# Taking a scheduled kernel into hand-made issue order: HGRN2 attention and an ELU MLP on one TensorE

## The chip, the cores and the metric

The kernel runs on one core of one Trainium2 chip. The metric is the device time of one execution in microseconds (us); where several executions are compared, the median is given with the lowest and the highest, and the number of executions. Engines are called as in the profile: PE is TensorE's matmul, PEld its weight load, DVE is VectorE, ACT is ScalarE, POOL is GpSimd, SP issues the DMAs. The granted clock is the share of TensorE's full clock that the profile records.

## The reference

The program computes a gated linear attention (a decaying 48x48 state for each head) and feeds its output as tokens into a two-layer MLP with ELU.

```python
q, k, v, f_logit          # (4, 8, 768, 48) float32 each
x     : tokens 3072, d_model 384, d_ff 2048
# attention
f = 1 / (1 + exp(-f_logit))
for t in range(768):
    state = f[:, :, t, :, None] * state + k_t outer v_t
    y[:, :, t] = q_t @ state
# MLP on x = y as (3072, 384)
h = x @ w_in                                   # 384 -> 2048
g = where(h > 0, h, exp(min(h, 0)) - 1)
return (g @ w_out).astype(float32)             # 2048 -> 384
```

The two weight matrices are float32 draws multiplied by a float64 scalar, so they arrive as 64-bit words. The kernel makes 32-bit weights of them itself; that is the "word split" below.

## The kernel before

The program works on 12 units of 256 tokens. In the outer loop, stage m runs the MLP of unit m and, threaded between its steps, the attention of unit m+1. Each of a stage's 16 steps is an "up" (six float32 matmuls into `psH`, two records each in the trace, so x12; then ACT, ACT and DVE make `gg`, and from the third stage on four DVE sums prepare the next operand) or a "down" (`psM`).

```python
def up(P):
    m, j = divmod(P, NP)
    ph = ps.tile([128, 2, U], FP32, tag="h", name=f"psH{m}_{j}", bufs=2)
    ...                                                       # six matmuls psH <- wi, xt: 2 tiles x 3 rows
    nc.scalar.activation(g[:], ph[:], AF.Relu, scale=-1.0)
    nc.scalar.activation(g[:], g[:], AF.Exp, scale=-1.0)
    nc.vector.scalar_tensor_tensor(out=g[:], in0=g[:], scalar=-1.0, in1=ph[:], op0=ALU.add, op1=ALU.max)
    if m >= DIRECT:                                           # DIRECT = 2
        ...                                                   # four tensor_tensor "sums"
```

The attention of a unit: decays (scan, reciprocal, product for each of four head pairs), transposes of k, `advance` (the outer products, into the PSUM banks a0 and a1), the chunk states on DVE, `scores` (again a0 and a1) with the causal mask, and `outputs` (a0 and a1 once more). So these three groups of matmuls take turns at the same two banks. The DVE instructions stood inside the functions whose matmuls they follow:

```python
def scores(u):
    ...                                       # 32 matmuls psS (64 records)
    for r in range(2):
        nc.vector.tensor_tensor(...)          # the mask, right behind the scores

def advance(u):
    ...                                       # 32 matmuls psU (64 records)
    for c in range(NC - last):
        stepped(u, c, ...)                    # the state operations, right behind them

def attention(u):
    return {
        3: [lambda: transposed(u, 0, "a0"), lambda: transposed(u, 1, "a1")],
        6: [lambda: advance(u)],
        8: [lambda: scores(u)],
        10: [lambda: outputs(u)],
        12: [lambda: carried(u)],
    }
```

The word split of one weight tile has one ACT and three DVE instructions:

```python
nc.scalar.activation(raw.bitcast(I32)[:, 0::2], raw.bitcast(U32)[:, 0::2], AF.Copy, scale=2.0**-29)
nc.vector.tensor_scalar(out=bits[:], in0=hi, ..., op0=ALU.logical_shift_left, op1=ALU.bitwise_and)
nc.vector.tensor_tensor(out=bits[:], in0=bits[:], in1=rnd, op=ALU.add)
nc.vector.scalar_tensor_tensor(out=to.bitcast(I32), in0=rows(hi), scalar=-(2**30), in1=rows(bits[:]),
                               op0=ALU.bitwise_and, op1=ALU.bitwise_or)
```

Issue order is made by hand in the preamble and stage 0 alone. From there the scheduler may move instructions on each engine:

```python
start.enter_context(tc.manual_schedule())
...                       # preamble
for m in range(NU):
    ...
    if m == 0:
        start.close()     # the scheduler orders what follows
        combine()
```

Of the kernel before, what the change touches and what calls it, by code (L numbers as in the profile page):

```python
# [10 lines left out]
U32 = mybir.dt.uint32  # L11
AF = mybir.ActivationFunctionType
# [343 lines left out]
def fast(ctx: ExitStack, tc: tile.TileContext, q, k, v, f_logit, w_in, w_out, out, flag):  # L356
# [14 lines left out]

# [17 lines left out]
    DIRECT = 2  # L389
    AHEAD = 7  # L390
# [35 lines left out]
    start.enter_context(tc.manual_schedule())  # L426
    blank(0, nc.vector, nc.gpsimd)
    load(0, nc.scalar)

    ident = cst.tile([128, 128], FP32, name="ident")  # L430
# [14 lines left out]
    for i in range(1, NB):  # L445
        blank(i, nc.gpsimd)
    between = cst.tile([128, NW, HP], FP32, name="between")
    fine = cst.tile([128, HP, NC], FP32, name="fine")
    nc.vector.memset(fine[:], 1.0)
    py = ps.tile([128, HP, W], FP32, tag="a1", name="psY")  # L450
    nc.vector.memset(py[:], 0.0)
# [15 lines left out]
    parts = [(0, 0), *((j + i, 1 - i) for j in range(NFT // 2 - 1) for i in (1, 0)), (NFT // 2 - 1, 1)]  # L467
# [19 lines left out]
    def rounding(n):  # L487

        if wide and n < NFT:
            raw = raws[n]  # L490
            nc.scalar.activation(
                raw.bitcast(I32)[:, 0::2], raw.bitcast(U32)[:, 0::2], AF.Copy, scale=2.0**-29
            )

    def convert(n):





        if not wide or n >= NFT:
            return
        j, out_ = parts[n]
        raw = raws.pop(n)
        rnd = raw.bitcast(I32)[:, 0::2]
        hi = raw.bitcast(I32)[:, 1::2]
        bits = sb.tile([128, 2 * DM], I32, tag="bits", name=f"bits{n}", bufs=1)
        nc.vector.tensor_scalar(
            out=bits[:], in0=hi, scalar1=3, scalar2=0x3FFFFFF8,
            op0=ALU.logical_shift_left, op1=ALU.bitwise_and,  # L510
        )
        nc.vector.tensor_tensor(out=bits[:], in0=bits[:], in1=rnd, op=ALU.add)
        to = wo[:, 2 * j : 2 * j + 2] if out_ else wi[:, :, j * 256 : (j + 1) * 256]

        def rows(x):
            return x.rearrange("p (k f) -> p k f", k=to.shape[1])

        nc.vector.scalar_tensor_tensor(
            out=to.bitcast(I32), in0=rows(hi), scalar=-(2**30), in1=rows(bits[:]),
            op0=ALU.bitwise_and, op1=ALU.bitwise_or,  # L520
        )
# [4 lines left out]

    def check(n):

        if not wide:
            return  # L530
        w = w_out if n % 2 else w_in
        flat = w.rearrange("a b -> (a b)").rearrange("(p i f) -> i p f", p=128, f=2 * DM)
        raw = area[:, 4 + n % (AHEAD - 4)]
        nc.sync.dma_start(out=raw, in_=flat[n // 2])
        for i, op in enumerate((ALU.min, ALU.max)):
            nc.vector.tensor_reduce(  # L536
                out=spans[:, i, n : n + 1], in_=raw.bitcast(FP32)[:, 1::2], axis=mybir.AxisListType.X,
                op=op, apply_absolute_value=True,
            )


    restart = cst.tile([128, HP, U], FP32, name="restart")
    nc.gpsimd.memset(restart[:], 0.0)

    def gates(u):
# [3 lines left out]
        for i in range(2):  # L549
            a = f[:, 2 * i : 2 * i + 2] if u else f[:, :, i * W : (i + 1) * W]  # L550
            nc.scalar.activation(a, a, AF.Exp, scale=-1.0)
            nc.scalar.activation(a, a, AF.Copy, bias=1.0)
            if u:
                nc.gpsimd.tensor_copy(restart[:, 2 * i : 2 * i + 2, ::C], a[:, :, ::C])
                nc.gpsimd.memset(a[:, :, ::C], 0.0)  # L555

    def growth(u, pairs, cols):

        t = qkf[u % NB]
        for p in range(pairs.start, pairs.stop):  # L560
            a = t["f"][:, p, cols]
            nc.vector.tensor_tensor_scan(  # L562
                out=a, data0=a, data1=restart[:, p, cols] if u else a,
                initial=1.0, op0=ALU.mult, op1=ALU.max,
            )
        k_ = t["k"][:, pairs, cols]
        nc.gpsimd.tensor_tensor(out=k_, in0=k_, in1=t["f"][:, pairs, cols], op=ALU.mult)  # L567

    def decays(u, pairs, cols):

        t = qkf[u % NB]
        nc.vector.reciprocal(pts[u][:, pairs, cols], t["f"][:, pairs, cols])  # L572
        q_ = t["q"][:, pairs, cols]
        nc.vector.tensor_tensor(out=q_, in0=q_, in1=pts[u][:, pairs, cols], op=ALU.mult)
# [7 lines left out]
    def prepare(u):  # L582

        gates(u)
        yield
        for i in range(2):
            for p in range(2 * i, 2 * i + 2):
                growth(u, slice(p, p + 1), slice(0, U))
            yield
        for p in range(HP):  # L590
            decays(u, slice(p, p + 1), slice(0, U))
            yield
        watch(u)

    def transposed(u, w, bank):

        pt = ps.tile([128, HP, 128], FP32, tag=bank, name=f"psT{u}_{w}")
        for p in range(HP):
            nc.tensor.transpose(pt[:, p, :], in_=qkf[u % NB]["k"][:, p, w * W : (w + 1) * W], identity=ident[:])  # L599
        kns[u, w] = sb.tile([128, HP, 128], FP32, tag="kn", name=f"kn{u}_{w}")  # L600
        nc.scalar.copy(kns[u, w][:], pt[:])

    def stepped(u, c, pu, end):

        s = sb.tile([128, HP, D], FP32, tag="state", name=f"state{u}_{c}", bufs=6)
        now = pu
        if u % UPB or c:
            nc.vector.tensor_tensor(out=s[:], in0=pu, in1=sts[u, c][:], op=ALU.add)
            now = s[:]
        decay = pts[u][:, :, end - 1 : end].broadcast_to([128, HP, D])  # L610
        nc.vector.tensor_tensor(out=s[:], in0=now, in1=decay, op=ALU.mult)
        sts[(u, c + 1) if end < U else (u + 1, 0)] = s

    def scores(u):
# [3 lines left out]
        pc = [ps.tile([128, NW, HP, C], FP32, tag=f"a{r}", name=f"psS{u}_{r}") for r in range(2)]  # L618
        for w in range(NW):
            for p in range(HP):  # L620
                for b in range(2):
                    cols = slice(w * W + b * C, w * W + b * C + C)
                    for r in range(2):
# [3 lines left out]
                        )  # L627
        for r in range(2):
            nc.vector.tensor_tensor(
                out=at[:, r].rearrange("k w p i -> k (w p) i"), in0=pc[r][:].rearrange("k w p i -> k (w p) i"),  # L630
# [3 lines left out]
    def advance(u):  # L634

        last = u % UPB == UPB - 1
        pu = [ps.tile([128, NW, HP, D], FP32, tag=n, name=f"psU{u}_{n}") for n in ("a0", "a1")]
        for w in range(NW):
            for p in range(HP):
                for r in range(2):  # L640
                    h = 2 * p + r
                    for b in range(2):
                        nc.tensor.matmul(  # L643
                            pu[b][FULL[r], w, p], lhsT=kns[u, w][FULL[b], p, FULL[r]],
# [3 lines left out]
        for c in range(NC - last):  # L648
            stepped(u, c, pu[c % 2][:, c // 2], (c + 1) * C)

    def outputs(u):


        pys[u] = [ps.tile([128, NW, HP, C], FP32, tag=f"a{b}", name=f"psY{u}_{b}") for b in range(2)]
# [41 lines left out]
    def first_scores(w):  # L696
        t = qkf[0]
        cols = slice(w * W, (w + 1) * W)
        at = ats[0, w] = sb.tile([128, 2, HP, W], FP32, tag="at", name=f"at0_{w}")
        pc = [ps.tile([128, HP, W], FP32, tag=f"m{2 + r}", name=f"psS0_{w}_{r}") for r in range(2)]  # L700
        for p in range(HP):
            for r in range(2):
                nc.tensor.matmul(
                    pc[r][:, p], lhsT=t["k"][HALF[r], p, cols], rhs=t["q"][HALF[r], p, cols],
                    start=True, stop=True,
                )
        for r in range(2):
            nc.vector.tensor_tensor(
                out=at[:, r], in0=pc[r][:], in1=causal[:].unsqueeze(1).broadcast_to([128, HP, W]),
                op=ALU.mult,  # L710
            )

    def first_advance(w):
        pu = ps.tile([128, HP, D], FP32, tag="a0", name=f"psU0_{w}")
        for p in range(HP):
            for r in range(2):
                h = 2 * p + r
                nc.tensor.matmul(
                    pu[FULL[r], p], lhsT=kns[0, w][:, p, FULL[r]], rhs=vs[0][:, w, h * D : (h + 1) * D],
                    start=(p == 0), stop=(p == HP - 1), skip_group_check=True,  # L720
                )
        stepped(0, w, pu[:], (w + 1) * W)

    def first_outputs(w):





        cols = slice(w * W, (w + 1) * W)  # L730
        q_ = qkf[0]["q"]
        if w == 0:
            xts[0] = sb.tile([128, HP, U], FP32, tag="xt", name="xt0", bufs=3)
        at = ats.pop((0, w))
        for part in range(2 if w else 1):
            for i in range(2 * NKT):
                j, r = divmod(i, 2)
                n = slice((j - 1) * PAD, (j + 1) * PAD)
                v0 = (2 * NKT + r) * D
                nc.tensor.matmul(  # L740
                    py[64 * r + 32 : 64 * r + 64, j, :],
# [241 lines left out]
```

## Time and profile before

| | before |
|---|---|
| median of 3 runs | 623.61 us (621.86 to 624.21) |
| span of the profiled execution | 620.9 us |
| PE busy | 572.7 us (92%) |
| first up | 33.9 us |
| stage 0, stage 1 | 65.7 and 62.6 us |
| a late stage | 44.9 us, PE busy 44.90 |

The prediction below shows the busy shares, the slices and three stretches. Two more views matter for what follows. The first is the fine timeline of a late stage before, DVE alone; the columns are start in us, length in us, engine, line, operation, tiles and shapes, and in brackets idle time before it and what ended it.

```profile
362.35 0.36 DVE L608 TENSOR_TENSOR state<-psU_a,state 128x192 f32<-128x192 f32 x1 [0.34 <-PE psU_a L643]
...
367.23 0.63 DVE L797 SCALAR_TENSOR_TENSOR gg<-gg,psH 128x512 f32<-128x512 f32 x1
...
370.51 1.27 DVE L629 TENSOR_TENSOR at<-psS,twice 128x512 f32<-128x512 f32 x2
...
373.70 0.63 DVE L797 SCALAR_TENSOR_TENSOR gg<-gg,psH 128x512 f32<-128x512 f32 x1
```

The reader should see the order. The state operations, which read `psU_a` and start at 362.35, come ahead of the next `gg` (367.23), and the mask (370.51) ahead of the one after (373.70). Both banks are free long before PE wants them, as the PE timeline of the same stage shows, where no bracket stands:

```profile
367.29 1.16 PE L624 MATMUL psS<-q,k 48*64 48x64 f32 x64
...
373.45 1.16 PE L661 MATMUL psY<-at,v 64*64 64x64 f32 x64
```

The second is from the table of costly groups: the up (count, busy us, mean ns of one, idle time before it).

```profile
L790 PE MATMUL psH<-xt,wi 128*128 128x256 f32 x1152 | 275.2, 390 | 0.0
```

The up never waited for anything that the group counts (the last column is 0.0). The ACT conversion of 768 words (the old word split) took 900 ns in the median of its 16 instances (870 to 940).

### The profile page before, as it was taken

How to read it: one execution, taken by the hardware profiler on the slowest of the kernel's cores; microseconds unless marked ns; L12 is line 12 of the kernel's file. 1: busy time of each engine (PE TensorE's matmuls, PEld its weight loads, DVE VectorE, ACT ScalarE, POOL GpSimd, SP SyncE). 2: the span in 40 equal slices, each digit the busy share in tenths (PEclk: the TensorE clock that was granted, in tenths of full speed). 3: DMA queues.
4: the chain of work that ended last, by engine and by line, in shares of the span. 5: the costliest groups of instructions: out<-in, count | busy, mean ns of one | idle time of the engine just before them, and what ended most of it. 6: DMA issues, size and time to landing. Idle time of an engine off the chain costs nothing.

```text
span 620.9 us, 13009 instructions
## 1 busy us (share of the span) xinstructions
PE 572.7 (92%) x5402; PEld 499.3 (80%) x5402; DVE 413.4 (67%) x839; ACT 196.7 (32%) x352; POOL 59.1 (10%) x115
## 2 busy tenths in 40 slices
PE   2787699898999899999999999999999999999994
PEld 1556476675879899899999899999989989999993
DVE  6879999998699976667576675483493443532432
ACT  2254244233413323325314322323313313323220
POOL 7021003223001001002002001000000000000000
PEclk9887799979999999999999999999999999999998
DMA  8999709338682403003112112002000000000000
GB/s 187 250 253 246 184 3 197 64 84 261 221 279 79 159 32 87 26 26 86 44 28 69 41 27 59 27 26 59 25 2 8 26 2 8 26 3 8 27 0 31
DMA packets 31781, 50.78 MB, mean 82 GB/s; under 512 B 3520, under 2 KB 24544, under 8 KB 31712
## 3 DMA queue, kind: packets, MB, share of 16 engines
q1 hardware_dynamic: 31088, 49.26, 30.0%
q8 instruction: 44, 0.72, 0.5%
q10 hardware_dynamic: 624, 0.59, 0.4%
q14 instruction: 25, 0.20, 0.1%
HBM read 44.04 MB, written 4.72 MB: 79 GB/s over the span
## 4 chain that ended last, share of the span: by engine, by line
PE 69%; DVE 14%; DMA 8%; issue 5%; POOL 1%; ACT 1%; SPq 0%; DVEq 0%; POOLq 0%
PE psH L790 33%; PE psM L840 25%; DMA area<-in_moe_w_in_dram 5%; DVE p L572 4%; PE psM L818 3%; DVE f L562 3%; DMA q<-in_q_dram 2%; PE psS L624 2%; DVE spans L536 2%; PE psU_a L643 2%; DVE gg L797 2%; PE psY L661 1%; PE psT L599 1%; PE psY L681 1%; DMA f<-in_f_logit_dram 1%
## 5 line engine op out<-in xcount | busy, mean ns | idle before, releaser
L790 PE MATMUL psH<-xt,wi 128*128 128x256 f32 x1152 | 275.2, 390 | 0.0
L790 PEld LDWEIGHTS psH<-xt,wi 128*128 128x128 f32 x1152 | 218.8, 194 | 32.2
L797 DVE SCALAR_TENSOR_TENSOR gg<-gg,psH 128x512 f32<-128x512 f32 x96 | 64.8, 676 | 162.5 <-ACT gg L796 132.4
L795 ACT ACTIVATE gg<-psH 128x512 f32<-128x512 f32 x96 | 57.2, 596 | 323.6 <-PE psH L790 299.2
L840 PE MATMUL psM<-area,sums 128*128 128x192 f32 x480 | 91.3, 326 | 0.0
L572 DVE RECIPROCAL p<-f 128x256 f32<-128x256 f32 x48 | 82.5, 1734 | 0.3
L840 PEld LDWEIGHTS psM<-area,sums 128*128 128x128 f32 x480 | 80.2, 190 | 0.0
L840 PE MATMUL psM<-wo,gg 128*128 128x192 f32 x320 | 65.5, 327 | 3.5 <-DVE gg L797 3.5
L840 PEld LDWEIGHTS psM<-wo,gg 128*128 128x128 f32 x320 | 55.4, 190 | 8.3 <-DVE gg L797 4.7
L567 POOL TENSOR_TENSOR k<-k,f 128x256 f32<-128x256 f32 x48 | 39.7, 853 | 230.0 <-DMA k<-in_k_dram 196.0
L796 ACT ACTIVATE gg<-gg 128x512 f32<-128x512 f32 x96 | 60.6, 631 | 2.6
L818 PE MATMUL psM<-wo,gg 128*128 128x384 f32 x128 | 47.3, 516 | 3.3 <-DVE gg L797 3.3
L807 DVE TENSOR_TENSOR sums<-gg 128x128 f32<-128x128 f32 x160 | 42.5, 306 | 2.0
L818 PEld LDWEIGHTS psM<-wo,gg 128*128 128x128 f32 x128 | 25.3, 203 | 19.4 <-DVE gg L797 4.1
L562 DVE TENSOR_TENSOR_SCAN f<-f,restart 128x256 f32<-128x256 f32 x44 | 31.6, 761 | 11.6 <-POOL f L555 11.6
L840 PE MATMUL psM<-area,gg 128*128 128x192 f32 x160 | 39.1, 326 | 0.0
L840 PE MATMUL psM<-wo,sums 128*128 128x192 f32 x160 | 39.1, 326 | 0.0
L599 PE MATMUL psT<-ident,k 128*128 128x128 f32 x96 | 15.3, 298 | 18.3 <-POOL k L567 18.3
L536 DVE TENSOR_REDUCE spans<-area 128x1 f32<-128x768 f32 x32 | 29.3, 942 | 2.0 <-DMA area<-in_moe_w_out_dram 1.7
L599 PEld LDWEIGHTS psT<-ident,k 128*128 128x128 f32 x96 | 12.0, 151 | 21.3 <-POOL k L567 20.0
L840 PEld LDWEIGHTS psM<-area,gg 128*128 128x128 f32 x160 | 28.1, 190 | 0.1
L840 PEld LDWEIGHTS psM<-wo,sums 128*128 128x128 f32 x160 | 28.1, 190 | 0.0
(79 smaller groups left out, 427.5 us busy)
## 6 DMA issues: line engine op xcount, KB each, us to landing
area<-in_moe_w_out_dram SPq DMA_DIRECT2D x16, 768.0 KB, 7.7
area<-in_moe_w_in_dram SPq DMA_DIRECT2D x8, 768.0 KB, 5.9
v<-in_v_dram SPq DMA_DIRECT2D x12, 384.0 KB, 4.4
area<-in_moe_w_in_dram SPq DMA_DIRECT2D x16, 288.0 KB, 9.0
f<-in_f_logit_dram SPq DMA_DIRECT2D x23, 192.0 KB, 4.3
k<-in_k_dram SPq DMA_DIRECT2D x23, 192.0 KB, 3.9
q<-in_q_dram SPq DMA_DIRECT2D x23, 192.0 KB, 3.6
out_dram<-o SPq DMA_DIRECT2D x10, 384.0 KB, 2.5
```

Of the source, the lines that this page charges most:

```text
L536: nc.vector.tensor_reduce(out=spans[:, i, n : n + 1], in_=raw.bitcast(FP32)[:, 1::2], axis=mybir.AxisListType.X, op=op, apply_absolute_val ...
L562: nc.vector.tensor_tensor_scan(out=a, data0=a, data1=restart[:, p, cols] if u else a, initial=1.0, op0=ALU.mult, op1=ALU.max,)
L567: nc.gpsimd.tensor_tensor(out=k_, in0=k_, in1=t["f"][:, pairs, cols], op=ALU.mult)
L572: nc.vector.reciprocal(pts[u][:, pairs, cols], t["f"][:, pairs, cols])
L599: nc.tensor.transpose(pt[:, p, :], in_=qkf[u % NB]["k"][:, p, w * W : (w + 1) * W], identity=ident[:])
L790: nc.tensor.matmul(ph[:, i], lhsT=wi[:, kt, n : n + 128], rhs=xts[m][:, kt, :], start=(kt == 0), stop=(kt == NKT - 1),)
L795: nc.scalar.activation(g[:], ph[:], AF.Relu, scale=-1.0)
L796: nc.scalar.activation(g[:], g[:], AF.Exp, scale=-1.0)
L797: nc.vector.scalar_tensor_tensor(out=g[:], in0=g[:], scalar=-1.0, in1=ph[:], op0=ALU.add, op1=ALU.max)
L807: nc.vector.tensor_tensor(out=s[:, i], in0=x, in1=y, op=op)
L818: nc.tensor.matmul(pm[t][:], lhsT=g[:, i, t * 128 : (t + 1) * 128], rhs=wo[:, 2 * j + i, :], start=(j == 0 and i == 0), stop=(j == NP - 1 ...
L840: nc.tensor.matmul(pm[bank][:, half * DH : (half + 1) * DH], lhsT=x, rhs=y, start=first, stop=(j == NP - 1), skip_group_check=True,)
```

## The change

The intent: place every instruction of the whole program by hand, so that the front, where DVE is the full engine, can be packed more tightly. The parts are these.

- `manual_schedule` is closed only at the end of the program.
- Decays, state operations and the mask become functions with steps of their own (0 to 3, 7 and 9). Downs lag two ups behind instead of one.
- Unit 0 goes through the four-chunk form of the other units; the padding rows between its heads come from zero-padded columns.
- The word split is cut in two: `split` (two DVE instructions with one source each, one ACT conversion with a 16-bit output) and, a step or more later, `merge` (a 32-bit add that writes the weights).
- Smaller matters: the activation table is loaded first, the last output goes out in smaller writes, the banks of a down are taken in another order, `combine` is spread over stage 1, and the re-reading of weights for the range check is separated from the check.

```diff
+    nc.scalar.preload_act_table(AF.Exp)
...
-        nc.vector.tensor_tensor(out=bits[:], in0=bits[:], in1=rnd, op=ALU.add)
+        nc.vector.tensor_scalar(out=hi, in0=hi, scalar1=-(2**30), scalar2=None, op0=ALU.bitwise_and)
+        nc.scalar.activation(
+            raw.bitcast(U16)[:, 2::4], raw.bitcast(U32)[:, 0::2], AF.Copy, scale=2.0**-29
+        )
+
+    def merge(n):
...
-        nc.vector.scalar_tensor_tensor(
-            out=to.bitcast(I32), in0=rows(hi), scalar=-(2**30), in1=rows(bits[:]),
-            op0=ALU.bitwise_and, op1=ALU.bitwise_or,
-        )
+        nc.vector.tensor_tensor(out=to.bitcast(I32), in0=rows(bits[:]), in1=rows(hi), op=ALU.add)
...
     def attention(u):
+        kept = []
         return {
-            3: [lambda: transposed(u, 0, "a0"), lambda: transposed(u, 1, "a1")],
+            **{p: [lambda p=p: decays(u, p)] for p in range(HP)},
+            4: [lambda: watch(u)],
+            5: [lambda: transposed(u, 0, "a0"), lambda: transposed(u, 1, "a1")],
             6: [lambda: advance(u)],
-            8: [lambda: scores(u)],
+            7: [lambda c=c: step(u, c) for c in range(NC)],
+            8: [lambda: kept.append(scores(u))],
+            9: [lambda: mask(u, kept[0])],
             10: [lambda: outputs(u)],
...
             P = m * NP + s // 2
+            if m == 0:
+                split(s + 3)
+                merge(s + 2)
             for f in todo.get(s - (m == 0), ()):
                 f()
             if s % 2 == 0:
                 up(P)
-            elif P:
-                down(P - 1)
+            elif P >= LAG:
+                down(P - LAG)
...
-        if m == 0:
-            start.close()
-            combine()
...
-    down(NU * NP - 1)
+    for P in range(NU * NP - LAG, NU * NP):
+        down(P)
+    start.close()
```

## The prediction

Statements about the hardware that the trace of the kernel before does not show are cut from the prediction, each cut marked. Its sum: 141 + 537.5 + 5.2 + 8.5 = 692.2 us of span, 695 with the 2.7 of the offset, 715 with the 20 for the clock (not quite half of the 46, an estimate from the one gap of 2.15 us told there). DVE's order: the L508, L512 and L518 of a tile of stage 0 start at 54.22, 54.91 and 55.91 us. That each engine keeps the order of issue (step 4) was the premise. The clock: "did not" means that it stayed at 1.00, after 1.11 us of idle before 106.97 and after 1.33 before 252.56; but after 1.34 us before 180.43 the scores ran at 1.00 and the up behind them, from 183.2, at 0.53. The 1.28 us at 5.28 is the load of the activation table.

> **What bounds the kernel now.** The program works on 12 units of 256 tokens. Stage m runs the MLP of unit m in 16 steps: even steps are an "up" (12 matmuls psH, then two ACT instructions, a DVE instruction that makes gg and, from m=2, four DVE sums), odd steps a "down" (psM). The attention of unit m+1 is threaded between them. I began with the page's busy shares and slices.
>
> ```profile
> PE 572.7 (92%) x5402; PEld 499.3 (80%) x5402; DVE 413.4 (67%) x839; ACT 196.7 (32%) x352; POOL 59.1 (10%) x115
> ...
> PE   2787699898999899999999999999999999999994
> PEld 1556476675879899899999899999989989999993
> DVE  6879999998699976667576675483493443532432
> ```
>
> TensorE is full from the 13th slice on. Before that (the first 210 us) DVE is the full one. The table by stretches puts figures on it; its columns are the length, busy us (count) of PE, PEld, DVE, ACT and POOL, then granted clock, DMA share and GB/s.
>
> ```profile
> 33.90:99.60 65.70, 53.78 (x427) 39.00 (x425) 60.94 (x90) 27.65 (x45) 7.11 (x12) 0.88 0.71 164
> 99.60:162.20 62.60, 56.66 (x438) 41.24 (x437) 55.51 (x76) 23.70 (x46) 17.55 (x32) 0.92 0.60 159
> ...
> 350.30:395.20 44.90, 44.90 (x474) 41.20 (x474) 27.50 (x64) 13.05 (x24) 2.97 (x4) 1.00 0.14 39
> ```
>
> The late stage is perfect: PE busy 44.90 of 44.90 us at clock 1.00. Only the front can be won. The chain of waits gives 2.59 us for an up, 2.27 for a down from m=2, 2.6 for a direct down (m=0, 1). The attention of a unit costs PE about 6 us (44.9 - 8x4.86). So a floor stage is 46.7-47 us for m=0 and 1, where the trace has 65.7 and 62.6, and 44.9 later. Stage 2 lost about 6.7, all later ones together 2.5. With the first up at 33.9, some 44 us are on offer altogether: 7%.
>
> What the new kernel does in every stage I read from the fine timeline of a late stage, PE and then DVE (start, length, engine, line).
>
> ```profile
> 219.07 2.75 PE L790 MATMUL psH<-xt,wi 128*128 128x256 f32 x12
> 221.66 0.81 PE L840 MATMUL psM<-wo,gg 128*128 128x192 f32 x4
> ...
> 223.15 0.69 DVE L797 SCALAR_TENSOR_TENSOR gg<-gg,psH 128x512 f32<-128x512 f32 x1 [3.69 <-ACT gg L796]
> 223.87 0.49 DVE L807 TENSOR_TENSOR sums<-gg 128x128 f32<-128x128 f32 x2
> ...
> 224.60 0.29 DVE L807 TENSOR_TENSOR sums<-gg,sums 128x128 f32<-128x128 f32 x1
> 225.22 0.36 DVE L608 TENSOR_TENSOR state<-psU_a,state 128x192 f32<-128x192 f32 x1 [0.33 <-PE psU_a L643]
> ...
> 228.43 1.75 DVE L572 RECIPROCAL p<-f 128x256 f32<-128x256 f32 x1
> ```
>
> An up issues its last matmul by E = 221.66. gg starts at E+1.49 (ACT is between), the sums end at E+3.23. The eight state operations take 0.395 each (225.22 to 228.43, less one wait).
>
> [...] in stage 0, the part of the old program already issued by hand, DVE follows the source line for line. [...] Here 2.15 us of idle (150.5 to 152.6) was followed by a mean clock of 0.61 over 4.4 us[...]; idle of 1.1 and 1.3 us did not. [...] the shift of 768 words (L508) takes 0.61 us, the two-source L518 0.96. [...] the trace has 1.28 at 5.28 us, on the path, and the new kernel loads the table earlier.
>
> **The change part by part.**
> 1. Preamble. Table load off the path: -1.3. Extra memsets on DVE hold it until about 7.2. Then four pairs of scan, reciprocal, product: scan 0.65, reciprocal 1.73, product 0.42, say 2.8 each, last one near 18.7. Split, mask 1.3, three state steps 2.5, two batches of small matmuls 2.5, copies 0.5 and merge 1.0 bring the first up to 27.6 instead of 33.9: **-6.3**.
> 2. Word split. Old per weight tile: L508 0.61 + L512 1.00 + L518 0.96 = 2.57. New: two single-source operations, 0.6 each, + the 1.00 add = 2.2: 16x0.37 = 6 us of DVE saved. The 16 combos (16x0.55 = 8.8) move from stage 0 to 1, where DVE has room once later units' preparation is no longer hoisted there.
> 3. Stage 0 in the new order. DVE has 14 merges and 13 splits, 29 us, decays 11.2, steps 3.2, mask 1.3, gg 8x0.68: 50 us. Placed in order, PE waits for steps before scores and for the mask before outputs; I get its end at 88.7. Stage 1: floor 46.7 + 3 + 1.4 + small waits = 52, end 141. The old kernel had done the same work (16 ups, 14 downs) at 154.4: **-13.5**, front included.
> 4. Steady stages: what I think decides. Python order becomes issue order on each engine.
>  a. The steps stand in step 7, behind the gg and sums of the up in step 6. Their last read of psU is the seventh operation: E + 3.23 + 6x0.395 + 0.36 = E+5.96. PE has only one down (2.27) before scores in step 8, which need those two banks. PE idle: **3.7 us** a unit.
>  b. The mask stands in step 9 behind the gg of step 8: ready at E+3.23+1.27 = E+4.5; outputs in step 10 are reached at E+2.27. Idle: **2.2**.
>  c. Decays are in steps 0 to 3: 4x2.8 = 11.2, with two gg groups 2x1.75. DVE starts them 1.0 us into the stage (behind the last gg), so the adds that free the psM banks start at 16.0 and free bank 0 at 16.8. PE reaches the first down in step 5 at 13.2. Idle: **3.6**; **5.1** where a check (two reductions, 1.8) stands in step 15. In stage 2 only the transpose waits, 2.1.
>  Stage 2: 44.9+3.7+2.2+2.1 = 52.9. Stage 3: 54.4. Stages 4 to 10: 7x55.9 = 391.3. Stage 11: 38.9.
> 5. End: the two lagging downs 4.5, direct ones 0.7, tail 8.5 instead of 9.1 (smaller last writes).
>
> Sum: 141 + 537.5 + 5.2 + 8.5 = 692 of span; the old median is 2.7 above its profiled span, so 695. Then cold clock: 27 gaps of 2 us or more, each worth up to 1.7 (0.39x4.4), 46 in all; slower PE partly only fills the next wait, so I count not quite half, 20. **Prediction 715 us.**
>
> The old trace shows one such wait already, where steps came late before scores in stage 0:
>
> ```profile
> 72.51 0.45 PE L624 MATMUL psS<-q,k 48*64 48x64 f32 x2 [5.54 <-issue]
> 73.29 1.98 PE L624 MATMUL psS<-q,k 48*64 48x64 f32 x62 [0.34 <-issue]
> ```
>
> 5.5 us of idle, then 1.98 us for what takes 1.08 warm.
>
> **The rivals.** (i) The order is as good as the scheduler's, and only the front counts: 27.6 + 2x46.7 + 9x44.9 + 38.9 + 9 = 573, or 576 with the offset. For it: the change is full of small choices that look tuned, such as the reordered banks of the down, and the lag of two makes gg late without harm. Against: no lag helps scores, outputs and the first down, which wait for steps, mask and adds, not for gg. (ii) The DMA sets stage 0: 15.7 MB of weights and first inputs at the 250 GB/s of the slices is 63 us, so weights land near 66 us. That hides what the split saves but lies inside my 88.7; it would cost rival (i) a few us and mine nothing. (iii) DVE order hurts only in a and b, because c's decays run ahead: 695-41 = 654. (iv) Every gap is followed by a cold spell: 741.
>
> **Range and chances.** Rival (iii) with a better stage 0 gives 640, rival (iv) with errors in stage 0 gives 750: range 640 to 750. For faster by over 2% (under 611) all my waits would have to shrink to a third: 0.10, mostly for a mistake in my reading of the order. Within 2%: 0.06. Slower: 0.84.
>
> **What would show it.** First up near 27.6 us (step 1). Stage 0 ending near 89 and stage 1 near 141. In each stage from 3 to 10, PE idle before psS by 3-4 us, released by the state operations; before psY by about 2, released by at; before the first psM by 3-5, released by the adds of o and u. Clock under 1.00 late in the span, PE share down from 92% to about 80%. Stages of 44.9 us would prove me wrong, and so would gg operations found behind the steps on DVE.

## The result and the profile after

| | before | after |
|---|---|---|
| median of 4 runs (before: the three above and one that ran beside the kernel after) | 622.74 us (621.45 to 624.21) | 757.61 us (755.32 to 760.88) |
| span of the profiled execution | 620.9 us | 759.1 us |
| mean granted clock | 0.966 | 0.908 |

The ratio is 1.217 (95% interval 1.211 to 1.223). Ratios in this document are the mean time of one kernel's runs over the mean time of the other's of the same rounds, so they are not quite the ratio of the medians quoted. The output was correct. The changed kernel is 135 us slower; the prediction had said 715 us, some 91 us slower, and its range ended at 750.

The page of the kernel after, busy shares, the slices and two of the costly groups (busy us, mean ns, idle before and what ended it):

```profile
PE 620.6 (82%) x5562; PEld 535.1 (70%) x5562; DVE 415.8 (55%) x849; ACT 218.0 (29%) x356; POOL 50.0 (7%) x118
...
PE   1654899898898797797898799689779779789896
...
PEclk9977999999899898898899789899889889889999
...
L769 PE MATMUL psH<-xt,wi 128*128 128x256 f32 x1152 | 304.9, 420 | 27.1 <-DVE wi L530 27.0
...
L516 ACT ACTIVATE area<-area 128x768 uint16<-128x768 uint32 x16 | 30.7, 1934 | 22.0 <-DVE area L515 18.9
```

PE's share fell from 92% to 82%, and the loss lies in every part of the span, not only in front: 14 of the 40 slices have a 9 in the PE row, where 31 had one before, and the clock row is below 9 in many late slices. The same 1152 matmuls of the up now take 420 ns instead of 390, and they waited 27 us for the merge that writes `wi`, where before the column said 0.0. The ACT conversion, now with a 16-bit output at every fourth half word, takes 1.93 us instead of 0.90 with a 32-bit one.

The table by stretches shows stages 0, 1 and 2 and a late one. Stage 0 is counted from its first up to that of stage 1, the others have the length from one stage's output copies to the next's; the windows of stages 1 and 2 lie 9.9 us ahead of these copies, so that stage 1 begins with its first up. The columns are the length, then busy us (count) of PE, PEld, DVE, ACT and POOL, the granted clock, the DMA share and GB/s.

```profile
33.10:111.40 78.30, 52.94 (x409) 37.65 (x410) 49.38 (x77) 42.60 (x44) 3.53 (x8) 0.85 0.58 138
111.40:164.10 52.70, 49.68 (x425) 36.43 (x424) 26.99 (x45) 16.07 (x31) 3.54 (x8) 0.97 0.24 52
164.10:218.50 54.40, 48.73 (x439) 41.32 (x438) 26.98 (x59) 14.88 (x28) 3.81 (x8) 0.94 0.16 33
409.48:471.18 61.70, 51.91 (x474) 46.35 (x473) 33.74 (x73) 15.47 (x30) 3.59 (x8) 0.89 0.24 60
```

Stage 0 takes 78.3 us although DVE, the full engine of the old front, is busy for only 49.4 of it. Stage 1 did become shorter (52.7 against 62.6). The late stage takes 61.7 instead of 44.9: PE is idle for 9.8 us of it and is busy 7.0 us longer with the same 474 matmuls, at a clock of 0.89.

The same late stage in the fine timeline, PE:

```profile
416.71 0.44 PE L590 MATMUL psT<-ident,k 128*128 128x128 f32 x2 [2.92 <-POOL k L577]
418.91 1.62 PE L819 MATMUL psM<-wo,gg 128*128 128x192 f32 x4 [1.76 <-DVE u L829]
...
432.85 0.29 PE L621 MATMUL psS<-q,k 48*64 48x64 f32 x2 [2.73 <-issue]
433.68 1.34 PE L621 MATMUL psS<-q,k 48*64 48x64 f32 x62 [0.53 <-DVE state L605]
434.95 4.30 PE L769 MATMUL psH<-xt,wi 128*128 128x256 f32 x12
...
443.07 0.29 PE L658 MATMUL psY<-at,v 64*64 64x64 f32 x2 [1.54 <-DVE at L629]
...
444.75 4.52 PE L769 MATMUL psH<-xt,wi 128*128 128x256 f32 x12
```

Three places have a wait, and after each of them in this stage PE is slow. Before the first down, the transposes wait for k and the down for the adds that free its banks (`u`); then its first four records take 1.62 us, where a down at full clock has 0.81 (granted clock 0.50 from 418.91 to 423.66). Before the scores PE stands still until the state operations have read the banks; the up behind it takes 4.30 instead of 2.86 (clock 0.66). Before the outputs it waits for the mask, and the next up takes 4.52 (clock 0.62).

DVE in the same stage tells why:

```profile
429.18 0.69 DVE L776 SCALAR_TENSOR_TENSOR gg<-gg,psH 128x512 f32<-128x512 f32 x1 [7.15 <-ACT gg L775]
...
433.18 0.36 DVE L605 TENSOR_TENSOR state<-psU_a,state 128x192 f32<-128x192 f32 x1
...
440.58 0.69 DVE L776 SCALAR_TENSOR_TENSOR gg<-gg,psH 128x512 f32<-128x512 f32 x1 [6.66 <-ACT gg L775]
...
442.24 1.28 DVE L629 TENSOR_TENSOR at<-psS,twice 128x512 f32<-128x512 f32 x2
```

DVE was idle for 7.15 us before this `gg`. The matmuls of `advance` had ended near 425.1, so for the last 4 us the state operations could have run. They waited all the same, because `gg` stands ahead of them in its order. Before the change the same eight instructions ran ahead of `gg`. Nothing was added to the work of the engine: only the order of its list changed, and with it the time at which a PSUM bank comes free for another engine. The mask at 442.24 stands behind a `gg` in the same way. (The bracket of the scores says `issue` for the first of the two banks; that wait ended at 432.85, 0.1 us behind the state operation that read this bank last, so it is the same wait.)

Stage 0 after, PE's timeline:

```profile
33.13 1.19 PE L769 MATMUL psH<-xt,wi 128*128 128x256 f32 x2 [1.75 <-DVE wi L530]
37.84 4.88 PE L769 MATMUL psH<-xt,wi 128*128 128x256 f32 x12 [3.52 <-DVE wi L530]
...
51.07 5.09 PE L769 MATMUL psH<-xt,wi 128*128 128x256 f32 x12 [8.35 <-DVE wi L530]
```

Ups wait up to 8.35 us for a merge. The counts show where: two records, then the wait, then twelve, which are the other ten of this up and two of the next. Each of these ups stops behind its first matmul. Except for the first 1.75 us, the merge that it waits for is not that of its own weight tile but one of a later tile: the second up needs the tile whose merge ended at 35.69 us and goes on at 51.07, right behind the end (51.01) of the fourth tile's merge. The experiment own_tiles below tests this.

### The profile page after: what moved, and what is told of

Read it like the earlier page. It is cut to its first block, busy times and chain, and to the rows that moved or that the text cites. A ratio compares the mean times of both kernels' runs of the same rounds, so it can differ in the third digit from the quotient of the medians. Undisturbed runs are those within 1.5% of the kernel's fastest.

```text
span 759.1 us, 13387 instructions
## 1 busy us (share of the span) xinstructions
PE 620.6 (82%) x5562; PEld 535.1 (70%) x5562; DVE 415.8 (55%) x849; ACT 218.0 (29%) x356; POOL 50.0 (7%) x118
## 4 chain that ended last, share of the span: by engine, by line
PE 52%; DVE 29%; DMA 7%; ACT 6%; issue 5%; POOL 0%; DVEq 0%; POOLq 0%
PE psH L769 28%; PE psM L819 15%; DVE p L575 8%; DMA area<-in_moe_w_in_dram 5%; DVE sums L786 4%; DVE gg L776 3%; DVE f L572 3%; ACT gg L774 2%; PE psM L797 2%; ACT gg L775 2%; DVE spans L547 2%; PE psS L621 2%; PE psY L658 2%; DVE at L629 2%; PE psY L678 2%
## 5 line engine op out<-in xcount | busy, mean ns | idle before, releaser
L769 PE MATMUL psH<-xt,wi 128*128 128x256 f32 x1152 | 304.9, 420 | 27.1 <-DVE wi L530 27.0
L769 PEld LDWEIGHTS psH<-xt,wi 128*128 128x128 f32 x1152 | 237.8, 211 | 70.3 <-DVE wi L530 28.0
L819 PE MATMUL psM<-area,sums 128*128 128x192 f32 x480 | 99.0, 346 | 0.0
L819 PEld LDWEIGHTS psM<-area,sums 128*128 128x128 f32 x480 | 87.7, 205 | 0.0
L819 PE MATMUL psM<-wo,gg 128*128 128x192 f32 x320 | 71.8, 351 | 13.4 <-DVE u L829 13.4
L577 POOL TENSOR_TENSOR k<-k,f 128x256 f32<-128x256 f32 x48 | 34.9, 727 | 133.8 <-DVE f L572 133.3
L621 PE MATMUL psS<-q,k 48*64 48x64 f32 x768 | 19.3, 248 | 28.5 <-issue 18.3
L590 PEld LDWEIGHTS psT<-ident,k 128*128 128x128 f32 x96 | 11.5, 149 | 43.8 <-POOL k L577 42.4
L621 PEld LDWEIGHTS psS<-q,k 48*64 48x64 f32 x768 | 16.8, 157 | 33.0 <-issue 32.9
L516 ACT ACTIVATE area<-area 128x768 uint16<-128x768 uint32 x16 | 30.7, 1934 | 22.0 <-DVE area L515 18.9
L562 POOL COPY restart<-f 128x8 f32<-128x8 f32 (+1 forms) x24 | 5.6, 232 | 473.3 <-ACT f L560 473.3
```

The lines of the kernel that those rows point to most:

```text
L516: nc.scalar.activation(raw.bitcast(U16)[:, 2::4], raw.bitcast(U32)[:, 0::2], AF.Copy, scale=2.0**-29)
L577: e.tensor_tensor(out=x[:, p], in0=x[:, p], in1=y, op=ALU.mult)
L590: nc.tensor.transpose(pt[:, p, w], in_=qkf[u % NB]["k"][:, 2 * h + p, w * W : (w + 1) * W], identity=ident[:])
L621: nc.tensor.matmul(pc[r][FULL[b], w, p], lhsT=t["k"][HALF[r], p, cols], rhs=t["q"][HALF[r], p, cols], start=True, stop=True,)
L769: nc.tensor.matmul(ph[:, i], lhsT=wi[:, kt, n : n + 128], rhs=xts[m][:, kt, :], start=(kt == 0), stop=(kt == NKT - 1),)
L819: nc.tensor.matmul(pm[bank][:, half * DH : (half + 1) * DH], lhsT=x, rhs=y, start=first, stop=(j == NP - 1), skip_group_check=True,)
```

## The experiments

Ten variants were run, all of them correct. Eight start from the kernel after and change it; two more go on from the best of those. Each call shares one chip and its own runs of the kernel before: 622.14 us in the first (median of 7), 620.34 us in the second (7), 622.66 us in the third (11).

**Theory.** The order on DVE makes PE wait at three places in each stage from the third on (before the first down, before the scores, before the outputs); each wait is followed by a stretch at low clock; and in stage 0 the ups wait for merges of later tiles. **Rivals.** The lag of two downs, the bank order, the form of unit 0 or the memory traffic of the word split cost the time, so that moving a few DVE instructions would not get it back; or stage 0 is set by DVE's amount of work or by the arrival of weights, and the waits on merges only stand in for that.

### steps_first: the state operations one step earlier

```diff
-            6: [lambda: advance(u)],
-            7: [lambda c=c: step(u, c) for c in range(NC)],
+            6: [lambda: advance(u), *(lambda c=c: step(u, c) for c in range(NC))],
```

> The new kernel with one edit: the eight state operations are issued in step 6, right behind the matmuls that feed them and ahead of the gg and sums of that step's up. Theory (issue order on DVE sets the waits): the idle of about 3.3 us before psS, in the trace 2.73 + 0.53, goes, and with it the slow clock of the scores and of the up behind them (4.30 us instead of 2.59), together some 5.3 us in each of the stages 1 to 10: 757 us falls by 45 to 55, to about 707. Rival (the wait only moves on, to the outputs or to the down that needs gg): less than 15 us is won. Right: stage 6 about 56 us instead of 61.7.

Measured: 708.76 us (708.52 to 708.92, 4 runs), ratio 1.140 to before (1.135 to 1.145). That is 49 us less than the kernel after, from moving eight DVE instructions per unit ahead of one `gg`. PE's timeline in a late stage of this run:

```profile
405.24 1.16 PE L621 MATMUL psS<-q,k 48*64 48x64 f32 x64
...
413.01 0.29 PE L658 MATMUL psY<-at,v 64*64 64x64 f32 x2 [1.54 <-DVE at L629]
413.61 1.16 PE L658 MATMUL psY<-at,v 64*64 64x64 f32 x62 [0.30 <-DVE at L629]
414.69 2.86 PE L768 MATMUL psH<-xt,wi 128*128 128x256 f32 x12
```

The wait before the scores is gone. The wait before the outputs is the same to the hundredth (1.54 and 0.30), but the up behind it now takes 2.86 instead of 4.52. Of the stages 2 to 10, eight are like that in this run and one has an up of 4.34 us; in the kernel after, where the longer gap lies some 8 us ahead, the up behind this wait took 4.2 to 4.5 us in six of the nine and 2.86 in the other three. So a wait of 1.84 us by itself seldom slowed the clock here; with the longer gap ahead of it, it did more often, but not always. The gain is more than the wait removed: ten units with 3.26 us each would be 33.

### mask_first: the mask in the step of its scores

```diff
-            8: [lambda: kept.append(scores(u))],
-            9: [lambda: mask(u, kept[0])],
+            8: [lambda: mask(u, scores(u))],
```

> The new kernel with one edit: the two mask operations are issued in step 8, right behind the scores and ahead of the gg and sums of that step's up. Theory: the idle of about 1.9 us before psY (1.54 + 0.30) goes and the up behind it, 4.52 us in stage 6, is warm again or at least partly: 2 to 4 us in each of the stages 1 to 10, a fall of 20 to 38 us. Rival (the wait only moves on): under 8 us.

Measured: 732.27 us (727.28 to 734.28, 4 runs), ratio 1.176 (1.169 to 1.183), 25 us less than after. The waits before the outputs are gone; those before the scores stay, and so does the slow up behind them (5.03 us instead of 2.86):

```profile
419.71 0.30 PE L621 MATMUL psS<-q,k 48*64 48x64 f32 x2 [2.74 <-issue]
...
422.45 5.03 PE L768 MATMUL psH<-xt,wi 128*128 128x256 f32 x12
...
429.68 1.16 PE L658 MATMUL psY<-at,v 64*64 64x64 f32 x64
```

### decays_early: most decays in the stage before

From unit 3 on the gates go to step 10 of the stage before, decays 0 and 1 to its steps 12 and 14, decays 2 and 3 to steps 0 and 2 of the stage; the range checks move from steps 13 and 15 to 9 and 11.

```diff
-            **{p: [lambda p=p: decays(u, p)] for p in range(HP)},
+            **({p: [lambda p=p: decays(u, p)] for p in range(HP)} if u < 3 else
+               {0: [lambda: decays(u, 2)], 2: [lambda: decays(u, 3)]}),
...
+            if m and m + 2 < NU:
+                if s == 10:
+                    gates(m + 2)
+                if s in (12, 14):
+                    decays(m + 2, s // 2 - 6)
```

> The new kernel with the third wait taken away alone: from unit 3 on, the gates are issued in step 10 and the first two decays in steps 12 and 14 of the stage before, the other two in steps 0 and 2, so that the adds that free the psM banks come earlier on DVE; the checks move from steps 13 and 15 to 9 and 11. Theory: DVE reaches the adds about 10.7 us into the stage, before PE reaches step 5 at 13.2; the idle of 4.9 us around the transposes and the slow clock of the down behind it (4.8 us for 2.3) go in the stages 3 to 10, 6 to 7.5 us each: a fall of 48 to 60 us, to about 703. Rival (DVE has too much to do anyway, 35 us of 44.9 in a full stage, and is late elsewhere): under 20 us, with new idle before psH or psY.

Measured: 693.58 us (693.18 to 696.98, 4 runs), ratio 1.119 (1.112 to 1.125), 64 us less than after, a little more than expected. It is the largest of the three. PE's timeline shows the transposes and the down in one go:

```profile
333.83 1.04 PE L590 MATMUL psT<-ident,k 128*128 128x128 f32 x8
334.70 0.82 PE L820 MATMUL psM<-wo,gg 128*128 128x192 f32 x4
```

### warm_gaps: the waits kept, PE busy in them

Eight, eight and four matmuls (40 records) whose result nobody reads are issued in the three gaps of each stage from the third on. They write the PSUM tile that the next up will overwrite.

```diff
-            8: [lambda: kept.append(scores(u))],
+            8: [lambda: warm(8 * u - 4, 8), lambda: kept.append(scores(u))],
```

(and the same in steps 5 and 10.)

> The new kernel with matmuls that nobody reads in the three idle places of each stage from 2 on (8 before the transposes, 8 before the scores, 4 before the outputs, about 3.5, 3.5 and 1.7 us), written to the buffer that the next up clears anyway; the order of the real work is the same. Theory (the slow matmuls behind each gap are the clock[...]): the waits stay, but the first down, the scores and the two ups run at 2.27, 1.1 and 2.6 us again; 5 to 6 us in each of nine stages, a fall of 40 to 55 us, granted clock near 1.00 in stage 6 instead of 0.89. Rival (they are slow because of what DVE and ACT read at the same time): no fall, or a rise by what the extra matmuls do not fit in. My prediction had counted 20 us for this term.

Measured: 722.16 us (719.99 to 724.28, 4 runs), ratio 1.162 (1.156 to 1.168). This is 35.5 us less than after, from more work. It is somewhat under the 40 us that was the least expected. (The profiled spans differ by 39.7 us, 759.1 and 719.4, because the profiled run of the kernel after was the slowest of its four.) The stretch of a late stage:

```profile
392.48:448.41 55.93, 54.59 (x514) 49.03 (x513) 33.74 (x73) 15.46 (x29) 3.60 (x8) 1.00 0.28 67
```

The clock is 1.00 and the stage takes 55.93 us, with every wait in place: the first down starts 8.53 us behind the start of the up ahead of it, exactly as in the kernel after, and the outputs from the second bank start at E + 4.58 in both (E is the time at which the last matmul of the up ahead has been issued). This separates the two terms of the loss: the waits are worth 55.93 - 44.9 = 11.0 us in a late stage, and the clock 61.7 - 55.9 = 5.8. The prediction's sum for such a stage without the clock was 55.9.

### own_tiles: eight weight tiles in place of one

No instruction is added or moved. Only the buffer `wi` of three rows by 2048 columns becomes eight buffers of three rows by 256.

```diff
-    wi = cst.tile([128, NKT, DFF], FP32, name="wi")
+    wis = [cst.tile([128, NKT, 256], FP32, name=f"wi{j}") for j in range(NP)]
```

> The new kernel with one edit: the weights of the up lie in eight buffers, one for each pair of word tiles, instead of one; no instruction is added or dropped. In the new kernel an up in stage 0 waits 2 to 8 us for the merge of a later weight tile, 27 us in all. Theory A (the wait is for a region that is taken too wide, because the merge is now a custom instruction that writes the weights itself): these waits go, and stage 0, 78.3 us from first matmul to last, falls by 12 to 22 us. Theory B (stage 0 is paced by the conversion on ACT, 1.93 us instead of 0.86 a tile, and the merges behind it): the ups wait somewhere else, and less than 5 us is won. Later stages stay at 52.7, 54.4 and about 61.

(The 0.86 us is half of a pair: in the kernel before two conversions from 41.66 took 1.72 us; the median of one is 0.90.)

Measured: 748.86 us (748.51 to 753.69, 4 runs), ratio 1.207 (1.200 to 1.214). Stage 0 took 67.0 us (33.96 to 100.95) instead of 78.3: 11.3 less, just short of theory A's 12. The median fell by 8.75 us, the profiled span by 12.1 (759.1 to 747.0); again the slow profiled run of the kernel after makes the difference. PE's timeline of the front:

```profile
33.96 8.43 PE L768 MATMUL psH<-xt,wi 128*128 128x256 f32 x24 [1.76 <-DVE wi L530]
...
57.36 0.69 PE L590 MATMUL psT<-ident,k 128*128 128x128 f32 x2 [4.94 <-POOL k L577]
```

The first two ups run in one go (24 matmuls), and the waits for merges fall from 27.0 us to 1.8 in the whole trace. So they were between different weight tiles: nothing but the buffer has changed. In the kernel before, the instruction that wrote `wi` was an ordinary two-source instruction; here it is the 32-bit add, which the trace records as a custom instruction (CUSTOM_DVE_ANT_0, over 1536 halves of words). Its output is three pieces of 256 columns, 2048 apart. The reading that fits is that its write is taken for the whole range from the first piece to the last, which holds columns of other tiles. The place where an up stops agrees: its first matmul reads the first row, ahead of where a later tile's range begins, and passes; its second reads the second row, which lies inside that range, and waits. Of these 25 us nearly half is lost to a new wait of 11.5 us before the transposes, for the products of k on POOL, which sit behind DVE's scans.

### right_order, right_order_tiles, right_order_old_split

These put the three edits of the order together (right_order), then add the eight tiles (right_order_tiles), or instead the old word split with one buffer (right_order_old_split). The last has 0.90 us conversions on ACT and an ordinary write of `wi`, but more work on DVE.

```diff
-        nc.vector.tensor_tensor(out=to.bitcast(I32), in0=rows(bits[:]), in1=rows(hi), op=ALU.add)
+        nc.vector.tensor_tensor(out=bits[:], in0=bits[:], in1=rnd, op=ALU.add)
+        nc.vector.scalar_tensor_tensor(
+            out=to.bitcast(I32), in0=rows(hi), scalar=-(2**30), in1=rows(bits[:]),
+            op0=ALU.bitwise_and, op1=ALU.bitwise_or,
+        )
```

> The three edits of order together (state operations in step 6, mask in step 8, decays early), the word split and its one weight buffer left as in the new kernel. Theory (the three waits and their slow clock are all that the later stages lost): each of the stages 2 to 10 takes 44.9 to 46 us as in the kernel before, clock 1.00, stage 1 about 48; with stage 0 still ending near 111 to 115 us that is 615 to 628 us, level with the kernel before. Rival (an in-order DVE loses more than that, which the first three waits hid): stages of 48 us or more, over 640 us.

> The three edits of order and the eight weight buffers, which took 9 us off the new kernel. Theory: the gains add, because stage 0 and the later stages share no wait: 9 to 13 us under the run with the order alone, 603 to 617 us, faster than the kernel before by 1 to 3%. Rival: stage 0 is bound by DVE once the order is right, and the buffers give under 4 us.

> The three edits of order with the word split of the kernel before (rounding into a 32-bit word on ACT, 0.86 us, add and a last operation that writes the weights, 2.57 us of DVE a tile), one weight buffer. It has neither the wide wait nor the 1.93 us conversions. Theory 1 (the 1.93 us on ACT delay gg in stage 0): 3 to 10 us under the run with the eight buffers. Theory 2 (DVE bounds stage 0): it is 2 to 6 us over that run, for 16x0.4 us more of DVE.

| | median us | ratio to before (95%) |
|---|---|---|
| before, same chip | 620.34 (619.08 to 625.47, 7 runs) | |
| right_order | 625.92 (624.97 to 626.82, 4 runs) | 1.008 (1.003 to 1.014) |
| right_order_tiles | 609.45 (608.63 to 610.01, 4 runs) | 0.981 (0.976 to 0.986) |
| right_order_old_split | 604.99 (603.72 to 606.07, 4 runs) | 0.973 (0.968 to 0.979) |

The three edits of order take the kernel from 757.61 to 625.92 us. Stages 2 to 9 are then 44.9 us each, as before the change. The lag, the bank order, the form of unit 0 and the new word split stayed in, so the rivals that blamed them fall. What is left against the kernel before lies in stage 0: the ups wait 31.3 us for merges in this run. The eight tiles take all but 1.8 us of it away (the run is 16.5 us shorter, where 9 to 13 were expected; whether it is 2% faster than before is unclear). With the old split 2.8 us are left, without new buffers, and the run is another 4.5 us shorter although DVE has 68.3 us of work from 33 to 110 us instead of 56.6. In the same stretch ACT's busy time falls from 44.6 to 32.4 us. In ACT's timeline the conversions stand ahead of the two instructions that make a `gg`. The new conversion is longer, and it also waits for the DVE instruction that writes the same words (22.4 us between 30 and 130 us of right_order_tiles); the old one waits for DMAs alone (8.1 us). With the old one, ACT's waiting for `psH` grows from 7.4 us to 29.9, DVE's `gg` waits 6.3 us for ACT instead of 18.2, and the 3.6 us for which PE itself waited for ACT's copies are gone. So the new split had moved work to an engine that then held up `gg`.

### flag_late and flag_late_turn_late

In stage 10 PE had waited 3.3 us for the reduction behind a range flag, a matmul `psF` that only has to come before the end. Flag_late is right_order_old_split with that matmul in step 8 of the last stage. The other one also sets the transposes, state operations, scores and outputs of unit 1 later by one or two steps, to give DVE time in stage 0.

```diff
+            if m + 1 == NU and s == 8:
+                send_flag()
```

> The right order with the old word split, and one edit: the matmul that sends the check's verdict is issued in step 8 of the last stage, not at the end of stage 10, where PE waits for a reduction on DVE (3.3 us idle before psF in the new kernel's trace; stage 10 takes 48.7 us where all others take 44.9). Theory: stage 10 takes 44.9 us, 3 to 4 us less in all, about 601. Rival: the wait only moves into stage 11, under 1 us.

> The same, and in stage 0 alone the transposes of unit 1 come two steps later and what follows them one or two. With the old place PE waits 12 us there for k (2.9 + 5.1 + 4.5 in the trace), because DVE still has decays and word tiles to do, while ups that need neither stand behind the transposes. Theory (PE can do ups and a down meanwhile; DVE sets the end of stage 0 near 91 us): 2 to 6 us less than the run beside it. Rival (DVE is so full that the stage ends when its work ends, and the later transposes only push the outputs back): within 1 us of it, or slower.

Measured: flag_late 602.06 us (600.30 to 602.61, 6 runs), ratio 0.966 (0.962 to 0.970), with stage 10 at 44.9 us instead of 48.7, as expected; flag_late_turn_late 606.35 us (605.76 to 607.37, 6 runs), ratio 0.974 (0.970 to 0.978). Flag_late is the best kernel. A stretch in its middle:

```profile
300.00:345.00 45.00, 45.00 (x458) 41.30 (x458) 34.11 (x72) 15.52 (x29) 3.52 (x8) 1.00 0.33 82
```

PE is busy for all of it, at clock 1.00. The other is a miss: later transposes took their own wait away, but a wait came back before the scores of unit 1, whose banks the state operations had yet to read: on DVE these stood behind word tiles and a `gg`, from the end of `advance` at 66.5 us until 75.54.

```profile
77.63 0.44 PE L624 MATMUL psS<-q,k 48*64 48x64 f32 x2 [8.34 <-issue]
```

What is left in front looks like DVE's load, which is not shown by a run: in flag_late DVE is busy 60.1 of the 66.8 us from 33.2 to 100, and PE waits 13.0 us for k, behind DVE's scans. No run here shortens that. The new preamble was not tried by itself.

## Why the prediction was right or wrong

**The direction and the mechanism were right.** PE's share was to fall to about 80% and was 82%; the three waits were to appear before scores, outputs and first down, and do; `gg` stands ahead of the steps on DVE. Their size was right too: in the late stage shown they are 4.7, 3.3 and 1.8 us where the working had 5.1, 3.7 and 2.2. (Of the first, 2.9 us lie before the transposes, which wait for k, and only 1.8 behind the adds that step 4c named.) From the timeline the scores' second bank was read to the end at 433.54, which is 5.86 us behind the last matmul of the up (427.68), where the working said E+5.96. The clean test is warm_gaps: 55.93 us for a late stage without the clock, where step 4 had summed 55.9. Stage 1 took 52.7 for 52, stage 2 (predicted 52.9 before any clock) 54.4, and the tail 8.6 for 8.5. Rival (i), the good order, is refuted by the result, and rival (iii), decays that run ahead, by decays_early: that wait was the dearest of the three. Rival (ii), the weights' arrival, did not set stage 0: own_tiles shortened it by 11.3 us with the same transfers.

**The time was wrong, 757.61 for 715, outside the range.** Two terms of the sum were mis-sized, each by some 20 us.

1. *The clock.* The step that failed is "slower PE partly only fills the next wait, so I count not quite half, 20". The whole figure in the same sentence, 46 us, was nearer. Stages 2 to 10 sum to 498.6 us in the prediction without the clock and to 542.8 in the trace (54.4, 423.9 for stages 3 to 9, 64.5; counted at the output copies). Of the 44.2 us between, 3.3 are the flag's wait in stage 10; about 41 are left. The direct test agrees: in warm_gaps the same stages sum to 504.0 us, 38.8 less. In the late stage shown, by the starts of the timeline, the first down took 4.75 us (418.91 to 423.66) instead of 2.27, and the two ups 4.14 and 4.36 instead of 2.59: 2.5, 1.5 and 1.8, together 5.8, as much as warm_gaps shows for the stage. In the stages 2 to 10 of the kernel after, the wait before the scores was 2.3 to 2.8 us, mostly with 0.5 us more between the banks, and the up behind it took 4.0 to 5.2 us instead of 2.86 each time. Little was absorbed: PE was busy 7.0 us longer than in a late stage before the change, and 5.8 of that shows in the length. The reason lies in the prediction's own formula: it puts the steps' end at E + 5.96 and the mask at E + 4.5, where E is the end of an up. A slow up moves E, and everything behind E moves with it; only slow work between E and the release could hide in a wait, and the downs that lie there run at full clock again (1.00 from 439.10 to 441.50). Rival (iv) was near with the clock.

2. *Stage 0.* Its end was predicted at 88.7 us and came at 111.4, so 22.7 of the error is here. Step 3 counted DVE's instructions and the two waits of the attention, and took the weights' writes as work to be placed. It did not ask which matmuls would be made to wait for a merge. The ups waited 27 us for merges, 25 of it for those of other tiles; own_tiles shows 11.3 us of stage 0's length come from it with the rest as it is, and 16.5 us of the total once the order is right. Step 2 was mis-sized as well: it counted what the split saves on DVE and passed over ACT, where each conversion went from 0.90 to 1.93 us, 16.5 us in all, and came to wait for DVE; right_order_old_split shows that going back to the old split is worth more than DVE's saving. And step 1 put the first up at 27.6 us; it came at 33.1, so the preamble gained 0.8 us, not 6.3. The estimate of 2.5 us for "two batches of small matmuls" was the largest miss there: the trace has them from 23.5 to 31.4 us.

Added up: 22.7 us from stage 0 and what comes ahead of it, 0.4 from stage 1, about 21 from the clock (41 against 20), 3.3 from the flag and -0.4 from the end are 47 us of span; the prediction's span was 712.2, the trace's 759.1. Against that, the offset of 2.7 us between median and span became -1.5, because the profiled run was the slowest of the four.

**The range was too narrow above.** Its upper end, 750, assumed that the clock might come out whole, as in rival (iv), and left 9 us for errors in stage 0. The two errors came together.

**What stays open.** The 4.5 us between right_order_tiles and right_order_old_split are put down to ACT by the waits alone; PE waits about as long for the write of `wi` in both (1.8 and 2.8 us). How much of it is the length of the conversion and how much its wait for DVE was not tested apart. That the custom instruction's write is taken for the whole range is read from own_tiles and the place where the ups stop; an ordinary write with the add's result in another buffer was only run together with the old split.

## What to carry to other kernels

When a kernel takes over the order from a scheduler, write down for each shared PSUM bank which instruction of another engine frees it, and put that instruction ahead of everything in its engine's list that waits for later work; here three such moves were worth about 132 us (757.61 to 625.92), where the change had lost 135. Count a PE gap of two to three microseconds, as they were here, with the slow matmuls behind it (5.8 us in a late stage), and do not discount them where the next wait is counted from the end of the same matmuls. When an instruction that writes part of a shared buffer is replaced by one of another kind, look in the trace at who waits for it, and give each part its own buffer if readers of other parts do (here 27.0 us of the ups' waits, 1.8 with separate buffers).
